# The recurrent part turned around and the Fourier part folded by symmetry, in an mLSTM cell with a Fourier mixing block

## The chip, the cores and the metric

The kernel runs on one core of a Trainium2 chip. The metric is the device time of one execution in microseconds (us). The engines are TensorE (PE in the profile, its weight loads PEld), VectorE (DVE), ScalarE (ACT), GpSimd (POOL) and SyncE (SP), which issues the DMAs.

## The reference

Two blocks in a row, all in float32. The first is a recurrent cell over 768 steps, for 4 batches and 8 heads of 40 features; the second mixes its output with a two-dimensional Fourier transform and a two-layer MLP.

```python
batch, n_heads, seq, head_dim = (4, 8, 768, 40)
for t in range(S):
    m_new = np.maximum(f_gate[:, :, t] + m, i_gate[:, :, t])
    f_stab = np.exp(f_gate[:, :, t] + m - m_new)
    i_stab = np.exp(i_gate[:, :, t] - m_new)
    m = m_new
    C = f_stab[:, :, None, None] * C + i_stab[:, :, None, None] * np.einsum('bhd,bhe->bhde', vt, kt)
    n = f_stab[:, :, None] * n + i_stab[:, :, None] * kt
    h_tilde = np.einsum('bhde,bhe->bhd', C, qt)
    nq = np.einsum('bhd,bhd->bh', n, qt)[:, :, None]
    denom = np.maximum(np.abs(nq), 1.0)
    y[:, :, t] = sigmoid(o_gate[:, :, t]) * h_tilde / denom
# x: y with the heads side by side, (4, 768, 320)
mixed = np.real(np.fft.fft(np.fft.fft(x, axis=1), axis=2))
u = x + mixed
un = (u - mean(u)) / np.sqrt(var(u) + 1e-06)          # over the 320 features
out = u + np.maximum(un @ w_ch1, 0.0) @ w_ch2         # 320 -> 1280 -> 320
```

## The kernel before

**Recurrent part** (`mlstm_chunk(b, c)`). The 768 steps of a batch are six chunks of 128. Inside a chunk the recurrence is written as a masked attention: `W` (key steps on the partitions, 8 heads times 128 query steps free) holds exp(a - M) under the causal mask, is multiplied by the scores `ps` = k·q, and `ph` = W·v1 is the part from within the chunk, v1 being v with a column of ones (so that the 41st column is nq). What came before the chunk is carried in `C` (40 x 41 for each head) and enters through `pn` = q·C, scaled by the decay of each query step. `pc` = k·(v1 scaled) updates C. In program order a chunk is: load `qk` (two DMAs), `kvt`, `Mb` (M broadcast to all partitions, 512 KB written); VectorE subtracts, GpSimd masks with `affine_select`, ScalarE takes one exp over 1024 columns; 8 matmuls ps, heads 0, 2, 4, 6 first and then 1, 3, 5, 7; VectorE multiplies W by ps; 4 matmuls pn, 8 matmuls ph with W as the standing operand; VectorE scales and adds them to `h1`; GpSimd scales v1 to `vw`; 8 matmuls pc; VectorE updates C; then `den` (three small VectorE operations), `so` times den on GpSimd, and `x` = h1 times so on VectorE.

**Fourier part** (the first half of `fnet(b)`). The sequence transform uses the sum and difference of the two halves of the sequence (`eo`, on GpSimd) for the even and the odd frequencies (`par`). `pz` and `pzt` multiply them by the table `ds_sb` (cosines beside sines, 386 or 384 columns), for the feature blocks of 128, 128 and 64; only frequencies up to 384 are computed, and copies in reverse order, the sine part negated, fill the mirrored ones into `Z` and `Zt`. The feature transform `pu` multiplies Z and Zt by `dd_sb`, five matmuls for each of six row blocks. `u` = pu + x, with its mean and variance by `bn_stats`.

**MLP** (second half of `fnet(b)`). `put` transposes u, `pm` multiplies it by the first layer (60 instructions in a group of three row blocks), ScalarE and VectorE take the relu in turn, `po` multiplies by the second layer, and the result is stored. The mean is taken out of the weights themselves (`center_weights`, matmul `pw`), and the third feature block is padded to 128 rows with zeros. The weights come as 64-bit floats and are converted from their bits by VectorE, ScalarE and GpSimd (`load_weights`).

The order at the top level is

```python
mlstm(0)
load_tables()
load_weights(cp); center_weights()
mlstm(1)
for b in range(B):
    if 1 < b + 1 < B:
        mlstm(b + 1)
    fnet(b)
```

and the framework's scheduler orders each engine's instructions at build time, by its own costs and by buffers that come free; so chunks of one batch stand between the transforms of another. All engines work their queues in that order. PSUM has four pools of two buffers each: `ps_s` for ps; `ps_h` for pn, ph and pc; `ps_f` for pz, pzt, pu and put; `ps_m` for pm, po and pw. `kvt` and `Mb` have three buffers, `qk` three, `W` two.

Of the kernel before, what the change touches and what calls it, by code (L numbers as in the profile page):

```python
# [10 lines left out]
FP = mybir.dt.float32  # L11
# [7 lines left out]
L = 128  # L19
# [7 lines left out]
TAIL = DM - 2 * L  # L27
TG = NT // 2
HALF = S // 2
NE = HALF // 2 + 1  # L30
NO = HALF // 2
M_INIT = -1.0e30
MASKED = -1.0e4


def backwards(ap, start, n):

    return bass.AP(tensor=ap.tensor, offset=ap.offset + start, ap=[list(ap.ap[0]), [-1, n]])
# [3 lines left out]
def kernel(  # L42
# [19 lines left out]
    mbp = ctx.enter_context(tc.tile_pool(name="mbp", bufs=3))  # L62
    wp = ctx.enter_context(tc.tile_pool(name="wp", bufs=2))
# [21 lines left out]
    C_bufs = [const.tile([L, NP, 2, D1], FP, name=f"C{n}") for n in range(2)]  # L85
    M_d = dram.tile([NT, BH, L], FP, name="M_d")


    with tc.tile_pool(name="gates", bufs=1) as gp:
# [11 lines left out]
        for t in qk_bufs + C_bufs:  # L101
            nc.gpsimd.memset(t, 0.0)

# [23 lines left out]
        nc.scalar.activation(out=g, in_=g, func=AF.Exp)  # L127
        dec = gp.tile([BH, BH // 2, NT], FP, name="dec")
        nc.vector.tensor_tensor(out=dec, in0=g[:, :, L - 1].unsqueeze(1).to_broadcast([BH, BH // 2, NT]),
                                in1=spread_sb[:, L:].unsqueeze(2).to_broadcast([BH, BH // 2, NT]), op=OP.mult)  # L130
        for c in range(NT):
            pt = ps_h.tile([L, 3, BH], FP, name="pt", tag="ph")
            for j, src in enumerate((a, wk, g)):
                nc.tensor.transpose(pt[:, j, :], src[:, c, :], ident[0:BH, 0:BH])
            nc.vector.tensor_copy(out=colT[:, c], in_=pt)
# [63 lines left out]
    def mlstm_chunk(b, c):  # L199
# [3 lines left out]
        C = C_bufs[b % 2]  # L203
# [5 lines left out]
        v1 = kvt[:, H * D:].rearrange("p (h d) -> p h d", d=D1)  # L209
# [4 lines left out]
        nc.vector.tensor_tensor(out=W, in0=colT[:, c, 0, heads].unsqueeze(2).to_broadcast([L, H, L]), in1=Mb,  # L214
                                op=OP.subtract)
        nc.gpsimd.affine_select(out=W, in_=W, compare_op=OP.is_ge, fill=MASKED, base=0, pattern=[[0, H], [1, L]],  # L216
                                channel_multiplier=-1)
        nc.scalar.activation(out=W, in_=W, func=AF.Exp)  # L218

        for hip in range(2):  # L220
            r = slice(hip * 64, hip * 64 + D)
            ps = ps_s.tile([L, NP, L], FP, name="ps", tag="ps")
            for p in range(NP):
                nc.tensor.matmul(ps[:, p, :], qk[r, 1, p, :], qk[r, 0, p, :], start=True, stop=True)  # L224
            Wv = W.rearrange("p (pr two) t -> p pr two t", two=2)[:, :, hip, :]
            nc.vector.tensor_tensor(out=Wv, in0=ps, in1=Wv, op=OP.mult)  # L226

        h1 = tp.tile([L, H, D1], FP, name="h1", tag="h1")
        if c > 0:
            pn = ps_h.tile([L, NP, 2 * D1], FP, name="pn", tag="ph")  # L230
            for p in range(NP):
                nc.tensor.matmul(pn[:, p, :], qk[:, 0, p, :], C[:, p].rearrange("p a b -> p (a b)"),  # L232
                                 start=True, stop=True)
            nc.vector.tensor_tensor(out=h1, in0=pn.rearrange("p pr (two d) -> p (pr two) d", two=2),
                                    in1=colT[:, c, 2, heads].unsqueeze(2).to_broadcast([L, H, D1]), op=OP.mult)
        ph = ps_h.tile([L, H, D1], FP, name="ph", tag="ph")
        for h in range(H):
            nc.tensor.matmul(ph[:, h, :], W[:, h, :], v1[:, h, :], start=True, stop=True)  # L238
        if c > 0:
            nc.vector.tensor_tensor(out=h1, in0=h1, in1=ph, op=OP.add)  # L240
        else:
            nc.vector.tensor_copy(out=h1, in_=ph)

        if c < NT - 1:
            vw = tp.tile([L, H, D1], FP, name="vw", tag="vw")
            nc.gpsimd.tensor_tensor(out=vw, in0=v1, in1=colT[:, c, 1, heads].unsqueeze(2).to_broadcast([L, H, D1]),  # L246
                                    op=OP.mult)
# [4 lines left out]
            for hip in range(2):  # L252
                r = slice(hip * 64, hip * 64 + D)
                Cv = C[r, :, hip, :]
                if c == 0:
                    nc.vector.tensor_copy(out=Cv, in_=pc[r])
                else:
                    d = decB[r, b * NP:(b + 1) * NP, c].unsqueeze(2).to_broadcast([D, NP, D1])
                    nc.vector.tensor_tensor(out=Cv, in0=Cv, in1=d, op=OP.mult)
                    nc.vector.tensor_tensor(out=Cv, in0=Cv, in1=pc[r], op=OP.add)  # L260

        nq = h1[:, :, D]
        den = tp.tile([L, H], FP, name="den", tag="den")
        nc.vector.tensor_scalar(out=den, in0=nq, scalar1=-1.0, scalar2=1.0, op0=OP.mult, op1=OP.max)  # L264
        nc.vector.tensor_tensor(out=den, in0=den, in1=nq, op=OP.max)
# [27 lines left out]
    def negate(eng, out, in_):  # L293
        if eng == 0:
            nc.scalar.mul(out, in_, -1.0)
        else:
            nc.vector.tensor_scalar(out=out, in0=in_, scalar1=-1.0, scalar2=None, op0=OP.mult)

    def fnet(b):
        x, _ = xs.pop(b)  # L300
        eo = eo_p.tile([L, 2, NT // 2, DM], FP, name="eo", tag="eo")
# [4 lines left out]
        Z = [z_p.tile([L, 2, S], FP, name=f"Z{ch}", tag=f"Z{ch}", bufs=1) for ch in range(2)]  # L306
        Zt = z_p.tile([L, S], FP, name="Zt", tag="Zt", bufs=1)
# [152 lines left out]
```

## Time and profile before

| | |
|---|---|
| median of 3 runs | 694.29 us (685.64 to 694.99) |
| profiled execution | 695.05 us, its span from first to last instruction 693.2 us |
| mean granted TensorE clock | 0.916 |
| busy share of the span | PE 89%, PEld 64%, DVE 41%, ACT 16%, POOL 19% |
| DMA | 45.60 MB, mean 66 GB/s |

The profile is of one execution. Its views give the busy time of each engine, groups of instructions by source line (L214 is line 214 of the kernel before), what each engine waited for, and the instructions in order of time. A row such as `L238 PE MATMUL ph<-kvt,W 128*128 128x41 f32 x384 | 71.2, 352 | 25.8 <-DVE W L226 24.1` reads: line, engine, operation, written tile and read tiles, sizes, count, busy us in total, mean ns of one, idle time of the engine just before, and what ended it. Matmuls are pipelined, so that the durations of neighbours overlap; the distance from one start to the next is what one costs in a stream. A timeline row gives the start and the length of a run of like instructions in us.

### The profile page before, as it was taken

To read this page: it belongs to the slowest core of one execution; us is meant where nothing else is said; L and a number is where in the kernel's file an instruction comes from. 1 tells how busy PE (TensorE), PEld (TensorE's weight loads), DVE (VectorE), ACT (ScalarE), POOL (GpSimd) and SP (SyncE) were. 2 spreads that over 40 slices of the span, in tenths; PEclk is the share of its full clock that TensorE was granted. 3 is DMA by queue.
4 is the path that set the end of the run, shared out by engine and by line. 5 is a ranking of instruction groups with operands and counts; after the bars stand their busy time and mean duration, and the time that the engine had idled before them with its cause. 6 is when DMAs were issued, how large, how long until landed. Compare 5 with 4: busy or idle time off the path is not lost.

```text
span 693.2 us, 6982 instructions
## 1 busy us (share of the span) xinstructions
PE 618.7 (89%) x2756; PEld 444.9 (64%) x2756; DVE 281.4 (41%) x558; ACT 110.1 (16%) x193; POOL 128.8 (19%) x113
## 2 busy tenths in 40 slices
PE   3879444259999999999999999999989999999998
PEld 3779423147877666687766676788756656666665
DVE  6454799995556311147343121255431011331110
ACT  4110323204102401001012021001121010110010
POOL 4230366672314100014040010021300000000000
PEclk9999999856579999997599999966999999999999
DMA  7436154542234100023220010120000000000000
GB/s 225 143 106 261 45 157 137 191 143 87 82 135 139 50 10 19 10 76 107 87 102 10 1 59 1 52 74 1 1 0 1 28 1 19 10 0 1 28 0 29
DMA packets 16113, 45.60 MB, mean 66 GB/s; under 512 B 1968, under 2 KB 5264, under 8 KB 15952
## 3 DMA queue, kind: packets, MB, share of 16 engines
q1 hardware_dynamic: 16080, 45.15, 19.8%
q8 instruction: 22, 0.36, 0.2%
q14 instruction: 11, 0.09, 0.0%
HBM read 41.11 MB, written 4.03 MB: 65 GB/s over the span
## 4 chain that ended last, share of the span: by engine, by line
PE 82%; DVE 11%; issue 3%; POOL 1%; ACT 1%; DMA 1%; POOLq 0%; DVEq 0%
PE pm L363 22%; PE po L375 19%; PE pu L340 9%; PE ph L238 9%; PE ps L224 7%; PE pz L318 6%; PE pn L232 4%; PE pzt L326 2%; DVE m L183 2%; PE pc L251 2%; DVE m L187 1%; PE put L356 1%; DVE e L182 1%; DVE e L188 1%; DVE e L179 1%
## 5 line engine op out<-in xcount | busy, mean ns | idle before, releaser
L363 PE MATMUL pm<-uT,w_sb 128*128 128x384 f32 x480 | 156.6, 487 | 0.6 <-ACT uT L357 0.6
L363 PEld LDWEIGHTS pm<-uT,w_sb 128*128 128x128 f32 x480 | 90.6, 190 | 62.4 <-ACT uT L357 0.8
L375 PE MATMUL po<-w_sb,hT 128*128 128x320 f32 x480 | 130.5, 432 | 0.0
L375 PEld LDWEIGHTS po<-w_sb,hT 128*128 128x128 f32 x480 | 91.2, 190 | 38.9
L238 PE MATMUL ph<-kvt,W 128*128 128x41 f32 x384 | 71.2, 352 | 25.8 <-DVE W L226 24.1
L238 PEld LDWEIGHTS ph<-kvt,W 128*128 128x128 f32 x384 | 68.7, 268 | 33.7 <-DVE W L226 21.8
L367 DVE TENSOR_SCALAR hT<-pm 128x384 f32<-128x384 f32 x40 | 22.3, 558 | 132.1 <-PE pm L363 132.1
L224 PE MATMUL ps<-qk 40*128 40x128 f32 x384 | 69.8, 382 | 0.3 <-DMA qk<-in_qkT 0.3
L224 PEld LDWEIGHTS ps<-qk 40*128 40x128 f32 x384 | 58.2, 266 | 6.8 <-issue 3.4
L378 DVE SCALAR_TENSOR_TENSOR ot<-po,rstd,u 128x320 f32<-128x320 f32 x24 | 13.2, 551 | 115.9 <-PE po L375 115.9
L340 PE MATMUL pu<-dd_sb,Z 128*128 128x320 f32 x192 | 56.0, 434 | 0.0
L218 ACT ACTIVATE W<-W 128x1024 f32<-128x1024 f32 x24 | 25.3, 1058 | 176.7 <-POOL W L216 176.6
L318 PE MATMUL pz<-ds_sb,eo 128*128 128x386 f32 (+1 forms) x96 | 48.1, 645 | 0.3 <-issue 0.3
L216 POOL TENSOR_SCALAR_AFFINE_SELECT W<-W 128x1024 f32<-128x1024 f32 x24 | 27.7, 1157 | 106.5 <-DVE den L264 62.2
L340 PEld LDWEIGHTS pu<-dd_sb,Z 128*128 128x128 f32 x192 | 36.1, 190 | 15.4 <-issue 0.6
L246 POOL TENSOR_TENSOR vw<-kvt,colT 128x328 f32<-128x328 f32 x20 | 15.9, 800 | 157.6 <-issue 127.1
L150 PE MATMUL pw<-w_sb,mean_sb 128*128 128x320 f32 x24 | 14.6, 774 | 30.6 <-POOL w_sb L189 23.9
L369 ACT ACTIVATE hT<-pm 128x384 f32<-128x384 f32 x40 | 19.6, 491 | 117.2 <-PE pm L363 117.2
L268 POOL TENSOR_TENSOR so<-so,den 128x320 f32<-128x320 f32 x24 | 21.0, 876 | 77.4 <-DVE den L266 77.4
L232 PEld LDWEIGHTS pn<-C,qk 128*128 128x128 f32 x160 | 31.4, 288 | 6.2 <-issue 4.9
L232 PE MATMUL pn<-C,qk 128*128 128x82 f32 x160 | 34.2, 384 | 0.5 <-DVE C L260 0.5
L226 DVE TENSOR_TENSOR W<-ps,W 128x512 f32<-128x512 f32 x48 | 32.2, 684 | 5.3 <-ACT W L218 2.8
(89 smaller groups left out, 504.9 us busy)
## 6 DMA issues: line engine op xcount, KB each, us to landing
Mb<-M_d SPq DMA_DIRECT2D x24, 512.0 KB
kvt<-in_kv SPq DMA_DIRECT2D x24, 324.0 KB
qk<-in_qkT SPq DMA_DIRECT2D x48, 160.0 KB
raw<-in_w SPq DMA_DIRECT2D x9, 640.0 KB
so<-in_o SPq DMA_DIRECT2D x4, 960.0 KB
out<-ot SPq DMA_DIRECT2D x24, 160.0 KB
ds_sb<-in_dft_s SPq DMA_DIRECT2D x1, 1155.0 KB
dd_sb<-in_dft_d SPq DMA_DIRECT2D x1, 800.0 KB
```

The costliest lines, as they stand in the source:

```text
L216: nc.gpsimd.affine_select(out=W, in_=W, compare_op=OP.is_ge, fill=MASKED, base=0, pattern=[[0, H], [1, L]], channel_multiplier=-1)
L218: nc.scalar.activation(out=W, in_=W, func=AF.Exp)
L224: nc.tensor.matmul(ps[:, p, :], qk[r, 1, p, :], qk[r, 0, p, :], start=True, stop=True)
L226: nc.vector.tensor_tensor(out=Wv, in0=ps, in1=Wv, op=OP.mult)
L232: nc.tensor.matmul(pn[:, p, :], qk[:, 0, p, :], C[:, p].rearrange("p a b -> p (a b)"), start=True, stop=True)
L238: nc.tensor.matmul(ph[:, h, :], W[:, h, :], v1[:, h, :], start=True, stop=True)
L268: nc.gpsimd.tensor_tensor(out=sc, in0=sc, in1=den.unsqueeze(2).to_broadcast([L, H, D]), op=OP.mult)
L318: nc.tensor.matmul(pz.rearrange("p a k -> p (a k)"), eo[:, par, j, ch * L:(ch + 1) * L], ds_sb[:, j, c0:c0 + 2 * n], start=(j == 0), stop= ...
L340: nc.tensor.matmul(pu, z, dd_sb[:, n, :], start=(n == 0), stop=(n == 4))
L363: nc.tensor.matmul(pu, w1_sb[:, ch, f * L:(f + 1) * L], uT[:, ch].rearrange("p c t -> p (c t)"), start=(ch == 0), stop=(ch == 2))
L367: nc.vector.tensor_scalar(out=ht, in0=pu, scalar1=0.0, scalar2=None, op0=OP.max)
L375: nc.tensor.matmul(po, hT[f][:, i * L:(i + 1) * L], w2_sb[:, f, :], start=(f == 0), stop=(f == NFF - 1))
```

## The change

Recurrent part:

- `W` is made in another order: ScalarE takes exp(a - M) straight from `Mb`, head by head (eight activations of 128 columns, a as the bias), and GpSimd's mask follows and fills with 0. VectorE's subtraction goes.
- The ps matmuls alternate between the two halves of the partitions (p outside, hip inside), into two PSUM tiles.
- `ph` is turned around: features on the partitions (two heads in 64 each), query steps free. v1, padded with zeros from 41 to 64 columns, is the standing operand, W the moving one. The old pn is added into the same PSUM tile: `C` (now 128 x 128 blocks, two alternating buffers a batch parity) stands, and `qg` moves, which is q times the decay (GpSimd), the decay broadcast by two new DMAs a chunk (`Gb`, from `G_d` in device memory). h1's scale and add on VectorE go.
- ScalarE copies ph to SBUF, four transposes on TensorE turn it back (`px`), and den and x read px.
- The product of C and its decay moves from VectorE to GpSimd.

Fourier part:

- `fe`: VectorE adds and subtracts feature d and feature 320 - d of eo, so that the cosine part has 161 features and the sine part 159. pz takes 128 of each (193 or 192 columns instead of 386 or 384), pzt the remaining 64 rows of each, alternating.
- `Z` has half its size. Mirrored frequencies are copied without negation; `dd_sb` holds the sine blocks with both signs instead.
- pu takes three matmuls for each row block instead of five.

The diff, cut to its core:

```diff
+    gbp = ctx.enter_context(tc.tile_pool(name="gbp", bufs=2))
...
-    colT = const.tile([L, NT, 3, BH], FP, name="colT")
+    colT = const.tile([L, NT, 2, BH], FP, name="colT")
+    fe = const.tile([L, 2, NT // 2, 2 * PAD], FP, name="fe")
-    C_bufs = [const.tile([L, NP, 2, D1], FP, name=f"C{n}") for n in range(2)]
+    C_bufs = [const.tile([L, NP, L], FP, name=f"C{n}") for n in range(4)]
+    G_d = dram.tile([NT, BH, L], FP, name="G_d")
...
+        nc.gpsimd.memset(fe, 0.0)
+        nc.sync.dma_start(out=G_d.rearrange("c p t -> p c t"), in_=g)
...
-        kvt = kvp.tile([L, H * (D + D1)], FP, name="kvt", tag="kvt")
+        kvt = kvp.tile([L, H * (D + VP)], FP, name="kvt", tag="kvt")
...
-        nc.vector.tensor_tensor(out=W, in0=colT[:, c, 0, heads].unsqueeze(2).to_broadcast([L, H, L]), in1=Mb,
-                                op=OP.subtract)
-        nc.gpsimd.affine_select(out=W, in_=W, compare_op=OP.is_ge, fill=MASKED, base=0, pattern=[[0, H], [1, L]],
+        for h in range(H):
+            nc.scalar.activation(out=W[:, h, :], in_=Mb[:, h, :], func=AF.Exp, scale=-1.0,
+                                 bias=colT[:, c, 0, b * H + h:b * H + h + 1])
+        nc.gpsimd.affine_select(out=W, in_=W, compare_op=OP.is_ge, fill=0.0, base=0, pattern=[[0, H], [1, L]],
                                 channel_multiplier=-1)
-        nc.scalar.activation(out=W, in_=W, func=AF.Exp)
+        ps = [ps_s.tile([L, NP, L], FP, name=f"ps{hip}", tag="ps") for hip in range(2)]
+        for p in range(NP):
+            for hip in range(2):
+                r = slice(hip * 64, hip * 64 + D)
+                nc.tensor.matmul(ps[hip][:, p, :], qk[r, 1, p, :], qk[r, 0, p, :], start=True, stop=True)
         for hip in range(2):
-            r = slice(hip * 64, hip * 64 + D)
-            ps = ps_s.tile([L, NP, L], FP, name="ps", tag="ps")
+            Wv = W.rearrange("p (pr two) t -> p pr two t", two=2)[:, :, hip, :]
+            nc.vector.tensor_tensor(out=Wv, in0=ps[hip], in1=Wv, op=OP.mult)
+        ph = ps_h.tile([L, NP, L], FP, name="ph", tag="ph")
+        if c > 0:
+            Gb = gbp.tile([L, NP, L], FP, name="Gb", tag="Gb")
+            for hip in range(2):
+                nc.sync.dma_start(out=Gb[hip * 64:hip * 64 + 64],
+                                  in_=G_d[c, b * H + hip:(b + 1) * H:2, :].unsqueeze(0).to_broadcast([64, NP, L]))
+            qg = gbp.tile([L, NP, L], FP, name="qg", tag="qg")
+            nc.gpsimd.tensor_tensor(out=qg, in0=qk[:, 0], in1=Gb, op=OP.mult)
             for p in range(NP):
-                nc.tensor.matmul(ps[:, p, :], qk[r, 1, p, :], qk[r, 0, p, :], start=True, stop=True)
...
+                nc.tensor.matmul(ph[:, p, :], C[:, p, :], qg[:, p, :], start=(p == 0), stop=False,
+                                 skip_group_check=True)
+        for p in range(NP):
+            for hip in range(2):
+                nc.tensor.matmul(ph[hip * 64:hip * 64 + 64, p, :], v1[:, 2 * p + hip, :], W[:, 2 * p + hip, :],
+                                 start=(c == 0 and p == 0), stop=True, skip_group_check=True)
+        hT = tp.tile([L, NP, L], FP, name="h", tag="h")
+        nc.scalar.copy(out=hT, in_=ph)
+        px = ps_h.tile([L, NP, L], FP, name="px", tag="ph")
+        for p in range(NP):
+            nc.tensor.transpose(px[:, p, :], hT[:, p, :], ident)
+        h1 = px.rearrange("p pr (two e) -> p (pr two) e", two=2)
...
-                    nc.vector.tensor_tensor(out=Cv, in0=Cv, in1=d, op=OP.mult)
+                    nc.gpsimd.tensor_tensor(out=Cv, in0=C[r, :, m], in1=d, op=OP.mult)
                     nc.vector.tensor_tensor(out=Cv, in0=Cv, in1=pc[r], op=OP.add)
...
+        nc.vector.tensor_copy(out=fv[:, :, 0:HALF_D + 1:HALF_D], in_=ev[:, :, 0:HALF_D + 1:HALF_D])
+        nc.vector.tensor_tensor(out=fv[:, :, 1:HALF_D], in0=near, in1=far, op=OP.add)
+        nc.vector.tensor_tensor(out=fv[:, :, PAD:PAD + HALF_D - 1], in0=near, in1=far, op=OP.subtract)
...
-            for ch in range(2):
-                pz = ps_f.tile([L, 2, n], FP, name="pz", tag="pf")
-                for j in range(NT // 2):
-                    nc.tensor.matmul(pz.rearrange("p a k -> p (a k)"), eo[:, par, j, ch * L:(ch + 1) * L],
-                                     ds_sb[:, j, c0:c0 + 2 * n], start=(j == 0), stop=(j == NT // 2 - 1))
-                copy(ch, Z[ch][:, :, k_dir], pz)
-                copy(ch, Z[ch][:, 0, k_mir], backwards(pz[:, 0, :], last, nm))
-                negate(ch, Z[ch][:, 1, k_mir], backwards(pz[:, 1, :], last, nm))
-            pz = ps_f.tile([L, n], FP, name="pzt", tag="pf")
+            pz = ps_f.tile([L, 2, n], FP, name="pz", tag="pf")
             for part in range(2):
                 for j in range(NT // 2):
-                    nc.tensor.matmul(pz[part * 64:part * 64 + TAIL], eo[:, par, j, 2 * L:DM],
+                    nc.tensor.matmul(pz[:, part, :], fe[:, par, j, part * PAD:part * PAD + L],
                                      ds_sb[:, j, c0 + part * n:c0 + (part + 1) * n],
                                      start=(j == 0), stop=(j == NT // 2 - 1))
...
+            copy(0, Z[:, :, k_dir], pz[:, :, 0:NO])
+            copy(1, Z[:, :, k_mir], backwards(pz, n - 1, NO))
+            pz = ps_f.tile([L, 1, n], FP, name="pzt", tag="pf")
+            for j in range(NT // 2):
+                for part in range(2):
+                    nc.tensor.matmul(pz[part * 64:(part + 1) * 64, 0, :], fe[:, par, j, part * PAD + L:(part + 1) * PAD],
...
-            for n, z in enumerate((Z[0][:, 0, m], Z[0][:, 1, m], Z[1][:, 0, m], Z[1][:, 1, m], Zt[:, m])):
-                nc.tensor.matmul(pu, z, dd_sb[:, n, :], start=(n == 0), stop=(n == 4))
+            for n, z in enumerate((Z[:, 0, m], Z[:, 1, m], Zt[:, 0, m])):
+                nc.tensor.matmul(pu, z, dd_sb[:, n + 2 if mir and n else n, :], start=(n == 0), stop=(n == 2))
```

More of the change, by code (lines that the diff above doesn't have):

```diff
@@ L27 @@
 TAIL = DM - 2 * L
+VP = 64
 TG = NT // 2
@@ L31 @@
 NO = HALF // 2
+HALF_D = DM // 2
+PAD = L + 64
 M_INIT = -1.0e30
-MASKED = -1.0e4
 def backwards(ap, start, n):
-    return bass.AP(tensor=ap.tensor, offset=ap.offset + start, ap=[list(ap.ap[0]), [-1, n]])
+    return bass.AP(tensor=ap.tensor, offset=ap.offset + start, ap=[list(d) for d in ap.ap[:-1]] + [[-1, n]])
 @with_exitstack
@@ L228, in mlstm_chunk @@
[L228 to L242, printed above, removed]
+        ps = [ps_s.tile([L, NP, L], FP, name=f"ps{hip}", tag="ps") for hip in range(2)]
[3 more added lines that the diff above has]
+                nc.tensor.matmul(ps[hip][:, p, :], qk[r, 1, p, :], qk[r, 0, p, :], start=True, stop=True)
```

68 lines of the change are left out of this document (35 added, 33 removed).

## The prediction

> **What bounds the kernel now.** The page's totals come first, for the engine that is full; then the busy time by stage, cut where TensorE's work changes. The columns of a stage are its length, busy time (and instructions) of PE, PEld, DVE, ACT and POOL, then TensorE's granted clock, DMA share and GB/s.
>
> ```profile
> PE 618.7 (89%) x2756; PEld 444.9 (64%) x2756; DVE 281.4 (41%) x558; ACT 110.1 (16%) x193; POOL 128.8 (19%) x113
> ```
>
> ```profile
> 14.00:79.00 65.00, 54.94 (x311) 50.79 (x310) 31.69 (x67) 7.67 (x8) 13.31 (x14) 1.00 0.43 151
> 79.00:147.00 68.00, 21.26 (x69) 13.50 (x69) 66.05 (x86) 20.67 (x25) 42.25 (x27) 0.91 0.50 157
> 147.00:208.30 61.30, 61.23 (x335) 49.08 (x335) 36.05 (x76) 13.41 (x18) 22.05 (x19) 0.63 0.31 103
> ...
> 302.00:353.80 51.80, 51.33 (x310) 39.49 (x308) 29.74 (x68) 7.85 (x14) 15.28 (x15) 0.70 0.30 98
> ...
> 446.00:495.00 49.00, 49.00 (x322) 40.91 (x321) 28.29 (x68) 5.87 (x12) 9.06 (x11) 0.72 0.13 38
> ...
> 598.50:617.00 18.50, 17.79 (x71) 12.38 (x72) 8.18 (x22) 1.51 (x7) 0.00 (x0) 1.00 0.00 1
> ```
>
> Stage A, 14 to 79 us, is the recurrent part of batch 0, with TensorE busy 54.94 of 65 us. B, to 147, converts the weights: VectorE is busy 66.05 of 68.00 us and TensorE waits. C (61.3 us), D (51.8) and E (49.0) each mix a recurrent batch with the sequence DFT of another, and TensorE has no gap. A last DFT runs alone, F, from 588.01 to 598.5. After each DFT comes a pu stage (the last row is the fourth) and an MLP stage, which the change leaves alone. So A, C, D, E, F and pu shorten as far as TensorE's work does.
>
> What that work costs is read from TensorE's timeline, from start to start: a chunk in A, a chunk in E, the last DFT.
>
> ```profile
> 53.91 0.65 PE L238 MATMUL ph<-kvt,W 128*128 128x41 f32 x2 [0.25 <-DVE W L226]
> 54.49 1.65 PE L224 MATMUL ps<-qk 40*128 40x128 f32 x6
> 56.06 3.21 PE L238 MATMUL ph<-kvt,W 128*128 128x41 f32 x14
> 59.20 0.78 PE L251 MATMUL pc<-vw,kvt 128*40 128x41 f32 x16
> 59.91 2.08 PE L224 MATMUL ps<-qk 40*128 40x128 f32 x10
> 61.92 2.00 PE L232 MATMUL pn<-C,qk 128*128 128x82 f32 x8
> 63.71 0.56 PE L238 MATMUL ph<-kvt,W 128*128 128x41 f32 x2
> ```
>
> ```profile
> 446.25 1.71 PE L224 MATMUL ps<-qk 40*128 40x128 f32 x16
> 447.89 1.12 PE L232 MATMUL pn<-C,qk 128*128 128x82 f32 x8
> 448.85 0.35 PE L238 MATMUL ph<-kvt,W 128*128 128x41 f32 x2
> 449.13 0.48 PE L224 MATMUL ps<-qk 40*128 40x128 f32 x2
> 449.55 1.76 PE L238 MATMUL ph<-kvt,W 128*128 128x41 f32 x14
> 451.23 0.51 PE L251 MATMUL pc<-vw,kvt 128*40 128x41 f32 x16
> 451.67 2.08 PE L224 MATMUL ps<-qk 40*128 40x128 f32 x14
> ...
> 588.01 3.41 PE L318 MATMUL pz<-ds_sb,eo 128*128 128x386 f32 x10
> 591.35 1.58 PE L326 MATMUL pzt<-ds_sb,eo 128*64 128x193 f32 x12
> 592.86 4.14 PE L318 MATMUL pz<-ds_sb,eo 128*128 128x384 f32 x12
> ```
>
> A matmul is two instructions here, so x16 is 8 matmuls. A chunk in A takes 9.8 us (53.91 to 63.71): ps 1.57+2.01, ph 0.58+3.14, pc 0.71, pn 1.79. In E the same takes ps 1.64, ph 0.28+1.68, pc 0.44, pn 0.96: 5.0 us. So A runs slow though its clock column reads 1.00; I go by the matmuls. C, D and E alternate, and their 0.63, 0.70 and 0.72 lie between a half and a whole.
>
> **The change, part by part.** *Recurrent part on TensorE.* ps alternates partitions 0 to 39 with 64 to 103, into two PSUM tiles. In ph, v1 (64 columns) stands and W (128) moves, in alternating output halves. pn becomes 4 matmuls of C on qg; 4 transposes come on top. Do halves overlap? pc alternates them now: x16 in 0.44 us is 28 ns each, where ps's 1.64/16 = 103 ns for 128 columns gives 33 ns for 41. pzt takes 1.51/12 = 126 ns for 193 columns, where pz's 3.34/10 = 334 ns for 386 gives 167. So yes, in part. The bounds for ps and ph are the whole time and half of it; I take half, nearest to pc, whose order is theirs. A slow chunk becomes ps 1.8, inter 1.8 (pn's row; 8 times ps's slow 0.2 would be 1.6), ph 1.8 (ps's columns, halved), transposes 4 x 0.22 = 0.9 (twice the 0.66/6 below), pc 0.7: **7.0 us**. A fast one: 0.8+1.0+0.8+0.45+0.44 = **3.5**. Saved: 2.8 slow, 1.5 fast.
>
> *Fourier part.* A batch's pz falls from 24 instructions of 386 columns to 24 of 193; pzt keeps its 24, in alternating halves; pu falls from 60 to 36.
>
> ```profile
> 550.80 0.66 PE put L356 x6
> ...
> 598.50 16.36 PE pu L340 x60
> ```
>
> pu: 24 fewer at 16.36/60 = 273 ns are 6.55 us, in four batches **26 us**, on the path. What is left, 9.8 us, still covers VectorE's 8.18 us of the stage. pz and pzt at full clock: 24 x 334 + 24 x 126 = 11.0 us become 24 x 167 + 24 x (84 to 126) = 6.0 to 7.0; I take 6.5, so 0.41 goes.
>
> *Other engines.*
>
> ```profile
> L318 PE MATMUL pz<-ds_sb,eo 128*128 128x386 f32 (+1 forms) x96 | 48.1, 645 | 0.3 <-issue 0.3
> L326 PE MATMUL pzt<-ds_sb,eo 128*64 128x193 f32 (+1 forms) x96 | 17.5, 391 | 0.0
> L214 DVE TENSOR_TENSOR W<-colT,Mb 128x1024 f32<-128x1024 f32 x24 | 30.2, 1258 | 2.5 <-DMA Mb<-M_d 2.5
> L216 POOL TENSOR_SCALAR_AFFINE_SELECT W<-W 128x1024 f32<-128x1024 f32 x24 | 27.7, 1157 | 106.5 <-DVE den L264 62.2 <-DVE W L214 20.2 <-DVE den L266 13.7
> L218 ACT ACTIVATE W<-W 128x1024 f32<-128x1024 f32 x24 | 25.3, 1058 | 176.7 <-POOL W L216 176.6
> L268 POOL TENSOR_TENSOR so<-so,den 128x320 f32<-128x320 f32 x24 | 21.0, 876 | 77.4 <-DVE den L266 77.4
> L246 POOL TENSOR_TENSOR vw<-kvt,colT 128x328 f32<-128x328 f32 x20 | 15.9, 800 | 157.6 <-issue 127.1 <-PE pc L251 25.7 <-DVE colT L135 4.2
> L259 DVE TENSOR_TENSOR C<-C,decB 40x164 f32<-40x164 f32 x32 | 12.0, 376 | 0.4
> L234 DVE TENSOR_TENSOR h<-pn,colT 128x328 f32<-128x328 f32 x20 | 9.9, 496 | 16.6 <-PE pn L232 16.6
> L358 ACT COPY uT<-put 64x128 f32<-64x128 f32 x24 | 6.2, 258 | 0.0
> L102 POOL MEMSET qk<- 128x1024 f32 x3 | 2.8, 962 | 0.1
> ```
>
> In a chunk VectorE loses L214, L234, the sum of h with ph (of L234's shape) and two L259: 1.26+0.50+0.50+0.75 = 3.0 us. ScalarE swaps one exp of 1.06 us for eight of 128 columns (bounds 0.13 us each, an eighth of L218, and 0.26, L358; I take 0.26, so 2.1) and gets a copy of 512 columns, by L218's rate at least 0.5, I take 0.6: +1.6. GpSimd gains qg, 512 columns at vw's 2.44 ns = 1.25 us, and two products for C of 164 = 0.8 us: from 1.16+0.80+0.88 = 2.8 to **4.9 us**. Beside TensorE's 7.0 that is hidden, beside 3.5 it is the bound. The fold adds two sums of 954 columns a batch on VectorE, by L214 about 2.4 us: beside the MLP for batches 1 to 3, in C for batch 0, where its 36 us lose 16. Uncovered it is 2.4 us a batch. Z needs fewer copies. Preparing gives GpSimd 3320 more columns of memset, at 962 ns per 1024 3.1 us, inside its 4.2 us wait for colT (L246).
>
> *The added waits.* The transposes wait for ScalarE's copy of ph. On TensorE the next chunk's ps, and in C, D and E a piece of pz, can stand between; else it idles 0.6 us, and 2.1 more if eight exps stand ahead of the copy. px holds one of the two ph buffers through den, so and x. I allow 2 us in A and 3 us in each of C, D, E.
>
> *DMA.* kvt grows by 92 KB and Gb adds 256 KB a chunk: A's 151 GB/s over 65 us, 9.8 MB, become 11.7 MB in 51 us, 229 GB/s, by A's ratio a share near 0.65. SP gets two more issues a chunk, behind Mb in its queue, and Gb's buffers free only when qg has read them; a late one holds the next chunk's qk and kvt loads, which run up to three chunks ahead. I count it hidden.
>
> *Stage B* keeps its VectorE and GpSimd conversion; the chunk and a half in it frees 4 us of VectorE and takes 3 of GpSimd: -1.
>
> **Sum.** Chunks by stage are ps instructions through 16:
>
> ```profile
> 147.00:208.30 61.30, 15.53 (x88) 0.63 0.31 103
> 302.00:353.80 51.80, 12.53 (x76) 0.70 0.30 98
> 446.00:495.00 49.00, 13.31 (x80) 0.72 0.13 38
> ```
>
> C has 5.5, D 4.75, E 5; A 6 and B 1.5 of the 24; the rest stand beside the MLP. pz and pzt took 65.6 us, less F's 10.5 are 55 in C, D, E; 0.41 of it is 22.5, 7.5 in each. By the clock a chunk saves 2.4 us in C and 2.2 in D and E. A: 6 x 2.8 - 2, less the missing pn and pc: -14. C: 5.5 x 2.4 + 7.5 - 3: -18. D: 4.75 x 2.2 + 7.5 - 3: -15. E: 5 x 2.2 + 7.5 - 3: -15. F: -4. pu: -26. The one and a quarter chunks beside the MLP, fast: -2. B: -1. Together -95 on the profiled execution's 695.05 us (span 693.2): **600 us**. The median shown, 694.29, lies 0.8 below that execution.
>
> **Rivals.** F, pu, the MLP chunks and B, -33 in all, are in each.
>
> *Clock up* (0.15): the new matmuls move 128 columns in both halves, and TensorE runs fast throughout, as at 446 us. Then GpSimd binds: A 6 x 4.9 + the 10 us in which TensorE now waits = 40; C 22+5.5 x 2.1 = 34, D 28, E 27 with handoffs: -25-27-24-22-33 = 564 us. For it: E's first chunk is fast behind dense work. Against: A is slow with TensorE 85% busy.
>
> *Clock down* (0.17): gaps keep it slow. C 5.5 x 7.0 + 2 x 6.5 = 51, D 46, E 48, A as forecast: -14-10-6-1-33 = 631. [...]
>
> *No overlap* (0.09): the halves take turns, and the change doesn't do what it says. A slow chunk is 3.6+1.8+3.2+0.9+0.7 = 10.2 us, a fast one 5.2. A +4, C -4, D -4, E -4 (pz and pzt save 0.36), rest -33: 654. [...]
>
> *Loop through GpSimd* (0.11): a chunk's select stands in the queue behind the last one's so: select 1.2, product 1.4, ph 1.8 to 3.7, copy 0.6, transposes 0.9, den 0.8, so 0.9, handoffs 1: about 10 us. A 60, C 55, D 48, E 50: -5-6-4+1-33 = 648. Against: the same loop has been there, and a chunk in A went at TensorE's 9.8 us.
>
> *Slower* (0.04): the same queue, and nothing overlaps; with exps 2.1 and x 0.7 it is 13.4 us a chunk. A 80, C 74, D 64, E 67: 58 more than their 227.1, less 33, is 720. It decides from a cycle of (227+33)/21.25 = 12.2 us. Against: W has two buffers, so exp and select can run a chunk ahead, and GpSimd has 2 us a chunk free.
>
> **Numbers.** Forecast, 580 to 620: 0.44. The range, 562 to 655, reaches to clock up and to the cases near 650; a spread of some us around those and the slower case leave out 2 in 10. Within 2%, about what a measurement of this kernel can tell from no change, would need the recurrent part to grow by some 40 us against the 55 that pu, F, the MLP chunks and the pz share give: faster 0.92, same 0.04, slower 0.04.
>
> **What would show it.** Right: pu x36 in 9.8 us; ps x16 under 2 us where slow; A near 51 us, C 43, D 37, E 34; MLP stages unmoved. Wrong: TensorE idle behind the copy of ph (ScalarE) or px's buffer (GpSimd's so); ps still above 3 us where slow; B longer.

## The result, and the profile after

The changed kernel took 633.0 us in the median of 4 runs (627.98 to 635.97), beside 694.55 us for the kernel before on the same chip: a ratio of 0.913, 95% interval 0.904 to 0.923. (Times are medians of all executions; the ratios are formed apart and leave out executions more than 1.5% above the fastest of their kernel, so that the two can differ a little.) The forecast was 600 us, a gain of 95; the gain was 61.5. The profiled execution took 635.97 us, its span is 634.3 us.

The totals of the page after, the line that answers to the first of before:

```profile
PE 535.2 (84%) x2750; PEld 372.2 (59%) x2750; DVE 225.0 (35%) x450; ACT 152.4 (24%) x366; POOL 166.5 (26%) x168
```

TensorE lost 83.5 busy us, but its share fell from 89 to 84%: some of what it lost came back as waiting. Where, is read from the moment at which the first pm of each batch starts, since the MLP behind it was left alone:

| stretch, by the two timelines of TensorE | before | after | measured | forecast |
|---|---|---|---|---|
| start to pm of batch 0 | 229.12 | 219.33 | -9.8 | -39.5 (A, B, C, one pu) |
| to pm of batch 1 | 143.53 | 125.58 | -18.0 | -22.5 (D, pu, chunks beside the MLP) |
| to pm of batch 2 | 142.48 | 122.16 | -20.3 | -22.5 (E, pu, chunks) |
| to pm of batch 3 | 102.04 | 91.22 | -10.8 | -10.5 (F, pu) |
| to the end of the profiled execution | 77.88 | 77.68 | -0.2 | 0 |

So 30 of the 36 us that are missing are missing before the first MLP. The busy times by stage, columns as before (length, PE, PEld, DVE, ACT, POOL, then granted clock, DMA share, GB/s):

```profile
14.00:79.00 65.00, 51.27 (x332) 41.40 (x332) 16.02 (x42) 18.88 (x55) 21.92 (x27) 0.79 0.56 179
79.00:147.00 68.00, 19.76 (x44) 11.50 (x44) 64.91 (x81) 25.11 (x42) 44.67 (x27) 0.50 0.47 146
147.00:197.50 50.50, 43.61 (x364) 35.11 (x364) 21.89 (x50) 15.13 (x42) 25.11 (x28) 0.76 0.51 167
292.00:330.70 38.70, 33.99 (x347) 27.00 (x346) 19.61 (x48) 17.75 (x50) 26.63 (x30) 1.00 0.65 192
418.80:455.00 36.20, 33.37 (x355) 26.93 (x353) 18.53 (x52) 11.67 (x33) 21.37 (x25) 1.00 0.21 67
```

The last two rows are D and E. They reach past the first wait of pu; up to the first pu, where D and E of the kernel before end, both are 33.1 us long (to 325.12 and 451.92) where 37 and 34 were forecast. They got there in another way: TensorE ran at full clock. Of the 4.7 and 2.8 us in which it is not busy in these rows, 3.7 and 1.2 are pu waiting for Zt. A fills its 65 us still and goes on to 82 us.

The timeline of TensorE in one chunk of A, from one inter-chunk product to the next:

```profile
62.21 2.08 PE L248 MATMUL ph<-qg,C 128*128 128x128 f32 x8 [2.78 <-POOL qg L246]
64.22 0.69 PE L252 MATMUL ph<-W,kvt 128*64 128x128 f32 x2
64.84 1.22 PE L233 MATMUL ps<-qk 40*128 40x128 f32 x4
65.99 1.97 PE L252 MATMUL ph<-W,kvt 128*64 128x128 f32 x14
67.89 1.65 PE L233 MATMUL ps<-qk 40*128 40x128 f32 x8
69.47 1.11 PE L258 MATMUL px<-ident,h 128*128 128x128 f32 x4
70.51 0.78 PE L268 MATMUL pc<-vw,kvt 128*40 128x41 f32 x16
71.21 0.80 PE L233 MATMUL ps<-qk 40*128 40x128 f32 x4
74.31 2.08 PE L248 MATMUL ph<-qg,C 128*128 128x128 f32 x8 [2.29 <-POOL qg L246]
```

From 62.21 to 74.31 it is 12.1 us: inter 2.01, ph 0.62 + 1.90, ps 1.15 + 1.58 + 0.80, px 1.04, pc 0.70, together 9.8, and 2.3 of waiting for qg. The 9.8 us are just what a chunk in A took before. What held qg before 62.21 stands in GpSimd's timeline:

```profile
59.14 0.99 POOL L276 TENSOR_TENSOR C<-C,decB 40x164 f32<-40x164 f32 x2 [7.41 <-DVE C L277]
60.22 0.72 POOL L284 TENSOR_TENSOR so<-so,den 128x320 f32<-128x320 f32 x1
60.90 1.26 POOL L246 TENSOR_TENSOR qg<-qk,Gb 128x512 f32<-128x512 f32 x1
62.11 1.09 POOL L225 TENSOR_SCALAR_AFFINE_SELECT W<-W 128x1024 f32<-128x1024 f32 x1
```

GpSimd has time to spare (7.41 us idle), but the next chunk's qg and select stand in its queue behind C's product, which itself waits for VectorE's C, and behind so.

The last Fourier transform begins, pu begins, and pu ends where put begins:

```profile
539.61 1.80 PE L337 MATMUL pz<-ds_sb,fe 128*128 128x193 f32 x10
...
546.01 1.34 PE L361 MATMUL pu<-dd_sb,Z 128*128 128x320 f32 x4
...
555.80 0.49 PE L377 MATMUL put<-ident,u 128*128 128x128 f32 x3
```

pu takes 9.79 us (546.01 to 555.80; 9.8 was forecast), pz and pzt together 6.4 (539.61 to 546.01; 6.5 was forecast). These were the well-sized parts.

For batch 0 and 1 the stage of pu nevertheless kept its length (from first pu to first pm 20.9 us before and 21.8 after in batch 0, 18.9 and 19.8 in batch 1). VectorE's timeline in batch 0's, and then in batch 1's, shows the fold of the next batch:

```profile
206.79 1.04 DVE L321 COPY fe<-eo 128x12 f32<-128x12 f32 x1 [2.77 <-POOL eo L314]
207.75 1.14 DVE L322 TENSOR_TENSOR fe<-eo 128x954 f32<-128x954 f32 x1
208.81 0.48 DVE L362 TENSOR_TENSOR u<-pu,x 128x320 f32<-128x320 f32 x1
...
327.18 1.23 DVE L321 COPY fe<-eo 128x12 f32<-128x12 f32 x1 [2.27 <-POOL eo L314]
328.31 2.10 DVE L322 TENSOR_TENSOR fe<-eo 128x954 f32<-128x954 f32 x1
330.33 0.34 DVE L307 COPY Zt<-pzt 128x192 f32<-128x192 f32 x1
```

VectorE's queue stands at fe until GpSimd has made eo (4.4 us); behind it wait the u that empties pu's PSUM buffer (TensorE idle 3.6 us) and the copy of Zt that pu reads (3.7 us). From the waits of TensorE (us in total, times, longest), the rows of these two and of qg:

```profile
PE ph L248 <- POOL qg L246: 5.7, 3, 2.8
PE pu L361 <- DVE Zt L307: 4.9, 2, 3.7
...
PE pu L361 <- DVE u L362: 3.6, 1, 3.6
```

### The profile page after: what moved, and what is told of

Its sections match the earlier page's. It is cut to its first block, busy times and chain, and to the rows that moved or that the text cites. A ratio compares the mean times of both kernels' runs of the same rounds, so it can differ in the third digit from the quotient of the medians.

```text
span 634.3 us, 7201 instructions
## 1 busy us (share of the span) xinstructions
PE 535.2 (84%) x2750; PEld 372.2 (59%) x2750; DVE 225.0 (35%) x450; ACT 152.4 (24%) x366; POOL 166.5 (26%) x168
## 4 chain that ended last, share of the span: by engine, by line
PE 59%; POOL 3%; DVE 2%; issue 1%; ACT 1%; POOLq 0%
PE pm L384 25%; PE po L396 20%; PE pu L361 5%; PE ps L233 2%; PE ph L252 2%; PE pz L337 1%; PE put L377 1%; POOL eo L314 1%; PE px L258 1%; POOL so L284 1%; PE ph L248 1%; PE pc L268 1%; POOL C L276 1%; DVE fe L322 1%; POOL vw L263 1%
## 5 line engine op out<-in xcount | busy, mean ns | idle before, releaser
L384 PEld LDWEIGHTS pm<-uT,w_sb 128*128 128x128 f32 x480 | 90.7, 190 | 62.5 <-ACT uT L378 0.8
L252 PE MATMUL ph<-W,kvt 128*64 128x128 f32 x384 | 41.5, 334 | 27.5 <-DVE W L236 26.7
L233 PE MATMUL ps<-qk 40*128 40x128 f32 x384 | 61.6, 355 | 1.9 <-DMA qk<-in_qkT 1.9
L223 ACT ACTIVATE W<-Mb,colT 128x128 f32<-128x128 f32 x192 | 59.4, 390 | 3.8 <-DMA Mb<-M_d 2.6
L233 PEld LDWEIGHTS ps<-qk 40*128 40x128 f32 x384 | 47.6, 233 | 14.3 <-issue 11.1
L252 PEld LDWEIGHTS ph<-W,kvt 128*64 128x64 f32 x384 | 30.2, 167 | 35.1 <-issue 22.5
L255 ACT COPY h<-ph 128x512 f32<-128x512 f32 x24 | 14.0, 584 | 137.6 <-PE ph L252 137.5
L361 PE MATMUL pu<-dd_sb,Z 128*128 128x320 f32 x96 | 32.9, 468 | 8.7 <-DVE Zt L307 4.9
L378 ACT COPY uT<-put 128x256 f32<-128x256 f32 x24 | 8.9, 370 | 115.9 <-PE put L377 115.8
L248 PE MATMUL ph<-qg,C 128*128 128x128 f32 x160 | 28.0, 330 | 10.0 <-POOL qg L246 5.7
L248 PEld LDWEIGHTS ph<-qg,C 128*128 128x128 f32 x160 | 24.4, 232 | 13.4 <-POOL qg L246 6.9
```

The lines of the kernel that those rows point to most:

```text
L223: nc.scalar.activation(out=W[:, h, :], in_=Mb[:, h, :], func=AF.Exp, scale=-1.0, bias=colT[:, c, 0, b * H + h:b * H + h + 1])
L233: nc.tensor.matmul(ps[hip][:, p, :], qk[r, 1, p, :], qk[r, 0, p, :], start=True, stop=True)
L248: nc.tensor.matmul(ph[:, p, :], C[:, p, :], qg[:, p, :], start=(p == 0), stop=False, skip_group_check=True)
L252: nc.tensor.matmul(ph[hip * 64:hip * 64 + 64, p, :], v1[:, 2 * p + hip, :], W[:, 2 * p + hip, :], start=(c == 0 and p == 0), stop=True, sk ...
L361: nc.tensor.matmul(pu, z, dd_sb[:, n + 2 if mir and n else n, :], start=(n == 0), stop=(n == 2))
L384: nc.tensor.matmul(pu, w1_sb[:, ch, f * L:(f + 1) * L], uT[:, ch].rearrange("p c t -> p (c t)"), start=(ch == 0), stop=(ch == 2))
```

## The experiments

Three theories had to be told apart for the missing part: the halves do not overlap; GpSimd's queue (C, so, qg, select, one after the other) sets the chunk; TensorE's clock, taken to follow the work in it, is the cause. Each kernel was timed beside the kernel before; its profile is of one execution.

**Each half of the change alone.** The first keeps the old recurrent part and takes the folded Fourier part; the second the reverse.

> The kernel before with the Fourier part of the change alone (fold, smaller pz, pu with three matmuls). Theory: pu gives 26 us, F 4 and the pz and pzt of C, D and E about 22, but each fold stands in VectorE's queue ahead of the last copy of Zt and of u, and TensorE waits for it as it does in the changed kernel (about 4, 8 and 6 us in C, D and E): about 660 us. Rival 1: the folds hide when the recurrent part is the old one, whose own work keeps TensorE busy: 643 us. Rival 2: the Fourier part is all of the gain: 633 us.

> The changed kernel with the old Fourier part, so the recurrent part of the change alone. Theory: it gains in D and E, where TensorE is fast and pz fills its gaps, about 10 us each, a few us in C, nothing in A: 665 to 672 us, with A as long as before (about 67 us). Rival: the recurrent part gains nothing anywhere, what D and E gained is the Fourier part: 690 us or more.

Fourier alone: 682.7 us, ratio 0.983 (0.970 to 0.995), above all three values expected. Recurrent alone: 667.4 us, 0.960 (0.949 to 0.971), as its theory said. By the ratios, single gains of about 12 and 28 us stand against 60 for both: the parts are far from adding up. The windows of the Fourier part alone, in C (pu starts at 218.9; two rows), D and E; the profiled execution, 685.07 us, is among the longest of its four (674.1 to 685.4):

```profile
147.00:200.00 53.00, 45.65 (x245) 41.41 (x245) 30.96 (x56) 9.65 (x8) 17.34 (x15) 0.50 0.24 80
200.00:218.80 18.80, 18.80 (x87) 15.98 (x86) 8.34 (x19) 2.12 (x5) 5.16 (x5) 0.55 0.32 109
310.00:352.50 42.50, 42.50 (x311) 35.76 (x310) 23.80 (x53) 3.60 (x6) 8.26 (x10) 0.92 0.33 103
440.00:500.50 60.50, 58.68 (x333) 51.53 (x331) 31.03 (x69) 5.46 (x7) 11.24 (x13) 0.58 0.14 40
```

With the old recurrent matmuls (41 or 82 columns) and half of pz gone, C ends 10.7 us later than before the change, at half clock, and in its last 18.8 us TensorE has no gap. As the fastest execution of this kernel is 11 us shorter than the profiled one, that length need not hold for all. E has become 11.5 us longer at 0.58; D went the other way, 9.3 us shorter at 0.92. The rows of the granted clock in 40 slices, of before, Fourier alone and recurrent alone, in this order, show where the slow slices lie:

```profile
PEclk9999999856579999997599999966999999999999
```

```profile
PEclk9999999555556879999899999955589999999999
```

```profile
PEclk9999999955899999999999999997989999999999
```

The fold alone makes more slices slow, early and late; the new recurrent part alone has hardly any in the later batches (its profile, too, is of a longer execution: 671.30 us of 659.8 to 673.0). The first slices read 9 in these kernels although ps took 0.2 us an instruction there, where it takes 0.11 in fast stretches, so A is judged by its matmuls: half clock, said of A, means that they take about twice their fast time.

**More of the old dense work.** To Fourier alone, each pz is issued a second time and overwrites the first: 96 more instructions of 193 columns.

```diff
-            for part in range(2):
+            for part in (0, 1, 0, 1):
```

> The Fourier part alone, with every pz matmul issued twice (the second time overwrites the first with the same), so TensorE has 96 instructions of 193 columns more, 16 us at full clock and 32 us at half. Theory: the Fourier part alone gained only 9 to 12 us because pz was the dense work that raised the clock in C, D and E, and with half of it these stages run slow (0.50 in most of C); with the work put back as mere load the clock comes back, and the time stays within 8 us of the Fourier part alone, 674 to 690 us, or falls. Rival, the clock does not depend on it: 16 to 32 us more, 699 to 715 us.

687.8 us, ratio 0.987 (0.979 to 0.994): 5.1 us more by the medians and about 3 by the ratios, where 96 instructions at 167 ns are 16 us and at half clock 32. The difference lies within the scatter of both, so that it bounds the cost rather than measures it. The added work cost less than its own time. The end of C shows how. Up to 205 us TensorE's timelines of the two kernels run alike, at half clock (both read 0.50 from 147 to 200 us); then come the last pz of C, first in Fourier alone, then with pz twice:

```profile
212.35 4.21 PE L331 MATMUL pz<-ds_sb,fe 128*128 128x192 f32 x12
```

```profile
211.99 4.17 PE L331 MATMUL pz<-ds_sb,fe 128*128 128x192 f32 x24
```

Twice the instructions take the same time, at full clock instead of half (170 ns an instruction from start to start against 345), and TensorE is without a gap in both. It is not so everywhere: E reads 0.58 without and 0.77 with the added work (440 to 500 us), but D, which reads 0.92 without, has slow matmuls with it: 14 instructions of ph took 3.13 us there (315.79 to 318.92) against 1.69 without (342.94 to 344.63). So more of pz can bring the clock up, and these two profiles do not say when it does.

**The halves of ps in turn**, so that less of ps can overlap.

```diff
-        for p in range(NP):
-            for hip in range(2):
+        for hip in range(2):
+            for p in range(NP):
```

> The changed kernel with the ps matmuls of one partition half after the other, as before, instead of alternating. Theory: alternating the partition halves never made them overlap (8 instructions take 0.86 us where fast and 1.58 where slow, 107 and 197 ns each, as before), so nothing changes: 633 us within 1.5%, and ps unchanged. Rival: the alternation does save something, and the time rises by 24 chunks times 0.8 to 1.6 us: 652 to 670 us.

630.3 us, 0.915 (0.908 to 0.921): nothing lost. I first read this as "ps does not overlap". That was wrong, as the filler kernels below showed: in the built program the framework's scheduler issues a ps matmul when its PSUM buffer comes free, and of 192 ps matmuls of the changed kernel only 65 stand right behind one of the other half; 66 stand behind one of their own and 61 behind other work. The alternation is in the source and hardly in the queue. Written in turn, 33 of 192 still stand behind one of the other half, so the two kernels differ by less than they seem to.

**The edges moved between engines.** Alone: ph's copy from ScalarE to VectorE; C's product and qg from GpSimd to VectorE; all three; those and so; and the fold's two sums from VectorE to GpSimd with the small copy on ScalarE.

```diff
-        nc.scalar.copy(out=hT, in_=ph)
+        nc.vector.tensor_copy(out=hT, in_=ph)
...
-            nc.gpsimd.tensor_tensor(out=qg, in0=qk[:, 0], in1=Gb, op=OP.mult)
+            nc.vector.tensor_tensor(out=qg, in0=qk[:, 0], in1=Gb, op=OP.mult)
...
-        nc.vector.tensor_tensor(out=fv[:, :, 1:HALF_D], in0=near, in1=far, op=OP.add)
+        nc.gpsimd.tensor_tensor(out=fv[:, :, 1:HALF_D], in0=near, in1=far, op=OP.add)
```

> The changed kernel with the copy of ph on VectorE instead of ScalarE. Theory: in stage A a chunk takes about 12 us because the queues tie it into a loop, and one knot is ScalarE, where the eight exps of the next chunk stand behind the copy of this one; untied, A falls by about 10 us, C and D by some: 615 to 622 us. Rival: A is bound by TensorE at its slow clock, so the time stays at 630 to 636 us and A at about 68 us.

> The changed kernel with the product of C and its decay and the product qg on VectorE instead of GpSimd, whose work on a chunk falls from 4.9 to 2.8 us. Theory: the other knot of the loop is GpSimd, where the select of a chunk stands behind C products, so and qg of the one before (TensorE waited 5.7 us for qg alone); untied, the time falls to 615 to 622 us. Rival, TensorE at its slow clock: 630 to 636 us.

> The changed kernel with the copy of ph, the C product and qg all on VectorE. Theory of the two knots: both gains, 603 to 615 us, stage A near 52 us. Rival, TensorE at its slow clock: 630 us, with stage A above 62 us and TensorE nearly without gaps in it. Second rival, VectorE becomes the knot (3.0 us a chunk more): above 636 us.

> The changed kernel with the copy of ph, the C product, qg and, beyond the last such run, the product so on VectorE, so that GpSimd has only the select and vw of a chunk (and eo), and ScalarE only the exps. Theory: what was left of the loop in A is the select, which stood in GpSimd's queue behind so of the chunk before (so at 62.1 us, select at 62.8, 12 us a chunk), although its exps were done at 48.3; with so gone the select runs a chunk ahead, a chunk in A falls from 12 to 9 us or less (TensorE's slow work is 8.9), A ends near 72 us instead of 85, and the time is 612 to 622 us. Rival: the cycle stays 12 us because TensorE's own order (ps halves between ph and px) holds it: A as before, 630 to 637 us.

> The changed kernel with the two sums of the fold on GpSimd instead of VectorE, and its small copy on ScalarE. Theory: TensorE waited at the end of C, D and E because the fold of the next batch held VectorE's queue, ahead of u and of the last copy of Zt; off that queue it costs nothing there: 615 to 622 us. Rival: the 4.4 us more on GpSimd delay the recurrent part's select and so, and the pu stage starts no sooner: 633 us or more.

| moved | us | ratio (95%) | last x of A starts |
|---|---|---|---|
| changed kernel | 633.0 | 0.913 (0.904 to 0.923) | 81.92 |
| copy | 645.6 | 0.926 (0.921 to 0.932) | 81.86 |
| C and qg | 633.6 | 0.910 (0.906 to 0.915) | 84.36 |
| copy, C, qg | 635.4 | 0.913 (0.907 to 0.918) | 84.53 |
| copy, C, qg, so | 632.2 | 0.911 (0.902 to 0.921) | 81.74 |
| fold on GpSimd | 637.5 | 0.921 (0.910 to 0.932) | 74.31 |

No move gains by itself: each of the five came out near its rival's value or above it, the copy above both values named for it (TensorE waited 8.6 us for u and 5.5 for the copy there). With so on VectorE too, GpSimd's select runs ahead, and still TensorE waits 2.30 us in a chunk (ph L248 at 62.88), now for VectorE's qg. So GpSimd's queue alone does not set A's length. With the fold on GpSimd, pu's waits fall from 8.5 us to 0.7, but those of ph for W rise from 26.7 to 30.4, behind the select, as the rival had it. There the profiled execution had a faster A, whose code is that of the changed kernel, and was also the fastest (628.46 us; the other three took 637.4 to 638.2): executions of one kernel differ by some 9 us here, a profile is of one of them, and A can run faster in one without any edit to it.

**The best of these together**: copy, C, qg and so on VectorE, ps in turn, the fold's sums on GpSimd.

> The same with the fold on GpSimd, which has room now, its small copy on ScalarE, and the ps matmuls in turn. Theory: the pu stages of batches 0, 1 and 2 lose their waits behind the fold (4, 4 and 3 us), ps in turn gives up to 3 us as it did alone: 8 to 12 us less than the run before it, 602 to 612 us. Rival: GpSimd's 4.4 us of fold a batch take the place of the waits, and nothing is gained.

621.0 us (618.6 to 622.4), 0.898 (0.892 to 0.905), 11 us below the same without the last two moves, the step that was expected (602 to 612 had been worked out from 612 to 622 for the run before, which took 632). With VectorE's queue free of the fold, pu no longer waits for u (6.8 us in the run before) or Zt; what ps in turn gave of the 11 was not separated. The first pu is at 192.2 instead of 197.5, but A still ends with its last x at 81.90.

**The clock, by itself.** Two matmuls of 512 columns are added to each chunk of batch 0, whose product nobody reads; first to the changed kernel, then to the last version.

```diff
+        if b == 0:
+            for n in range(2):
+                wm = ps_m.tile([L, NP * L], FP, name="warm", tag="pm")
+                nc.tensor.matmul(wm, ident, qk[:, n].rearrange("p a t -> p (a t)"), start=True, stop=True)
```

> The changed kernel, with two matmuls of 128 x 128 on 512 columns added to each of the six chunks of stage A (batch 0), their product read by nobody. By the rows of the Fourier part each costs 0.89 us at full clock and 1.77 us slow. Theory: stage A runs slow because its matmuls are short and leave gaps of 2 to 3 us a chunk; dense work keeps the clock up, ps 8 instructions falls from 1.57 to 0.86 us and a chunk from 12 us to 7 to 10 us although it holds 1.8 us more: stage A ends 12 to 30 us earlier, and the time is 605 to 621 us. Rival: TensorE's rate in A has nothing to do with what fills it, and the added matmuls only cost: 1.5 to 3.5 us a chunk, A ends 9 to 20 us later, 640 to 655 us. In between (time within 5 us of the changed kernel's): the gaps take the added work and the clock stays where it is.

> The version with copy, product of C, qg and so on VectorE, ps in turn and the fold's sums on GpSimd (621.0 us, stage A ending at 82.4 us), with the filler in stage A besides. In the profiled execution of the changed kernel with filler, stage A ended at 73.9 us instead of 82.4 and the first pu began 8.5 us earlier, but its median fell only by 3 us. Theory: stage A is TensorE at a clock that dense work raises, and in this version no GpSimd wait is left in its way: A ends near 70 to 75 us and the whole is 8 to 12 us shorter, 609 to 613 us. [...]

On the changed kernel: 630.1 us, 0.915 (0.905 to 0.925), no difference that the time can show, though in the profiled execution (626.9 us, its fastest) the last x of A starts at 73.45 instead of 81.92. As A reached 74.31 with the fold on GpSimd and no filler, that one profile does not show the filler's effect. On the last version: **608.1 us** (604.4 to 611.5, six runs), 0.877 (0.871 to 0.882), where no run of it without filler was below 618.6. The last x of A starts at 70.95 instead of 81.90, the first pu at 177.17 instead of 192.21. Twelve useless matmuls, at 0.9 to 2.0 us each, make the kernel 13 us faster. TensorE's timeline in A of the last version, without filler:

```profile
56.04 1.97 PE L252 MATMUL ph<-W,kvt 128*64 128x128 f32 x14
57.94 2.07 PE L233 MATMUL ps<-qk 40*128 40x128 f32 x8
```

and with it:

```profile
39.13 1.13 PE L232 MATMUL warm<-qk,ident 128*128 128x512 f32 x2
40.18 1.09 PE L256 MATMUL ph<-W,kvt 128*64 128x128 f32 x14
41.20 1.13 PE L232 MATMUL warm<-qk,ident 128*128 128x512 f32 x2
42.16 0.60 PE L262 MATMUL px<-ident,h 128*128 128x128 f32 x4
42.69 0.51 PE L272 MATMUL pc<-vw,kvt 128*40 128x41 f32 x16
43.13 1.71 PE L237 MATMUL ps<-qk 40*128 40x128 f32 x16
44.85 1.13 PE L252 MATMUL ph<-qg,C 128*128 128x128 f32 x8
```

The 14 instructions of ph take 1.90 us without (56.04 to 57.94), 1.02 with it (40.18 to 41.20). Without the filler ph is slow in four of the six chunks of A and partly slow in two; with it, slow in the fifth and partly in the second. The filler also moves the order (ps no longer stands between ph and px), so a part of the 11 us that A loses may be the order's; the instructions themselves are faster. In both filler kernels TensorE now waits for the load of Mb (1.89 and 1.43 us before the ph at 45.67 and 47.41 us), which the prediction had counted as hidden. The changed kernel with filler, whose ps stands in full alternation at this point of the queue, settles the first theory:

```profile
41.53 1.16 PE L237 MATMUL ps<-qk 40*128 40x128 f32 x16
42.62 1.16 PE L252 MATMUL ph<-qg,C 128*128 128x128 f32 x8
```

Sixteen in 1.09 us alternating (41.53 to 42.62), 1.72 in turn (43.13 to 44.85), both at full clock (px of the same chunk takes 0.53 us in each, where it takes 1.04 without filler at 59.94): halves of ps do overlap, to 0.63 of the time, where the queue lets them.

## Why the prediction was right, and where it failed

Direction and mechanism held: TensorE bounds the kernel, and C, D, E, F and the later pu stages, in which it has less to do, are shorter. The time is 33 us above the forecast, near the 631 us of "clock down" by another route: that rival had D and E at 46 and 48 us and A at 51; D and E took 33.1 each at full clock, and A kept its 65. The nearness is luck. One of the prediction's own signs of being wrong came: ps takes 3.5 us where slow, above its 3. By its steps:

- **pu, F, pz**: pu 9.79 us against 9.8, pz and pzt 6.4 against 6.5. Of the -26 for pu, batches 2 and 3 got theirs (their stages lost 5.0 and 6.5 us); batches 0 and 1 lost it again to the fold.
- **The fold** was counted as hidden on VectorE. Its work is small (L322 took 1.14 and 2.10 us); what the step missed is its place in an in-order queue, ahead of u and Zt and itself waiting for eo. "Uncovered it is 2.4 us a batch" priced the busy time and not the wait. Taken out of that queue it gained nothing alone; with ps in turn, in the kernel whose GpSimd had been relieved, it was worth 11 us.
- **The halves**: "I take half, nearest to pc". ph did come down, at full clock to 64 ns an instruction (16 in 1.03 us, from 306.80), where ps in turn takes 107 for as many columns. For ps the term of 1.8 us measured 3.5 in a chunk of A: overlap is real (0.63, not a half), but in the built queue only a third of ps stands behind the other half. Where two halves of 40 rows do alternate, these traces show 1.6 times the speed (1.09 us against 1.72 for sixteen).
- **The slow chunk**, 7.0 us in the sum, measured 9.8: ps +1.7, ph +0.7, inter +0.2, px +0.1. With 2.3 us of waiting, where 2 us had been allowed for the whole stage, a chunk of A is 12.1. **This is the failed step**: A was to give 14 us. Its last x and VectorE's first conversion operation, which begins B, are before and after:

```profile
76.25 0.49 DVE L179 TENSOR_SCALAR e<-raw 128x640 uint32<-128x640 uint32 x1
82.83 1.82 DVE L269 TENSOR_TENSOR x<-h,so 128x320 f32<-128x320 f32 x1
```

```profile
81.92 0.49 DVE L285 TENSOR_TENSOR x<-px,so 128x320 f32<-128x320 f32 x1 [0.84 <-POOL so L284]
82.32 0.48 DVE L186 TENSOR_SCALAR e<-raw 128x640 uint32<-128x640 uint32 x1
```

The last x is 0.9 us earlier, and B begins 6 us later, since the conversion now stands in the queue behind it. What one slow chunk was to save, 2.8 us, it did not save at all.
- **B** is then 4.4 us shorter (first conversion operation to the last correction of w_sb: 69.4 and 65.0), against -1. **C** gave 12.3 (62.5 to 50.2) of 18. Together with the 0.9 of pu's stage, 6.0 - 4.4 - 12.3 + 0.9 = -9.8, where -39.5 was forecast.
- **The clock** was held where it was in C, D and E, with both ways out as rivals. It rose to 1.00 in D and E, where a chunk takes 5.4 us (307.83 to 313.21) against a fast 3.5 in the sum, ps alone 1.8 against 0.8. That error and the clock cancelled: D and E came near their forecast by luck. In C it rose to 0.76. In A it stayed low for the later chunks (0.64 from 48 to 62 us, 0.50 from there to 79, with ps at 197 ns an instruction at 67.89). "Clock up" put A at GpSimd's 4.9 us a chunk; with filler, where the column reads 0.98 (14 to 48 us), a chunk took 7.0 us, filler included (34.05 to 41.09 in the changed kernel with it).
- **The rival through GpSimd** (648 us) had the queue right, select behind so, and the wait is there in A. But taking it away did not shorten A: at half clock TensorE's own 9.8 us come first, and the wait moves to the next engine (2.30 us for VectorE's qg).

What the terms of the sum hid: they were added as if independent. The clock ties them. With the fold alone it fell in C (0.63 before, 0.50 and 0.55 then) and E (0.72 before, 60.5 us at 0.58 then) and rose in D (0.70 to 0.92); with the new recurrent part alone D and E read 1.00 and 0.95. That the fold's missing work lowers it and the new matmuls raise it is the likely reading; the runs do not give the rule. A clock that rises with how busy TensorE is would fit the filler kernels (14 instructions of ph in 1.02 us with the filler, 1.90 without); C of the kernel before (61.23 of 61.30 us busy at 0.63) and of the Fourier part alone (18.80 of 18.80 at 0.55) speak against it, if busy means occupied. What in TensorE's work the clock follows, no run here tells; why A runs at half clock stays open with it.

One count of the prediction is off without consequence: preparing adds 3696 columns of memset by the tiles (2304 for fe, 1392 for C), not 3320.

## What to carry to other kernels

Price a stage of short matmuls at full and at half clock (ps took 107 and 197 ns an instruction here), not at the clock of the stage before the change alone, and expect two edits that change what TensorE does there not to add up (12 and 28 us alone, 60 together). An overlap that the source writes down must be looked for in the built queue (65 of 192 here), and an added operation is priced by what stands behind it in its engine's queue while it waits (pu lost 3.6 and 3.7 us behind the fold). Where a stage on the critical path runs at half clock and has gaps, a filler matmul into an unused buffer is a cheap test, and may be a gain (13 us here, and none that the time can show in the changed kernel itself).

## What was not expected of the hardware

- Useless work can pay: twelve matmuls of 512 columns took the best version from 621.0 to 608.1 us.
- TensorE without a gap can run near half clock (18.80 of 18.80 us at 0.55 in the Fourier part alone), and with gaps at full clock (33.37 of 36.20 us at 1.00 in E after the change).
- Two halves of ps in alternation took 68 ns an instruction against 107 in turn; the transposes, 4 instructions, took 0.58 us behind a ps of 109 ns an instruction (46.47 us after the change) and 1.04 behind one of 197 (69.47), so they slow down with it.
- The same sum over 954 columns on VectorE took 1.14 us in batch 0's stage and 2.10 in batch 1's, there beside a select and a product qg of GpSimd, which took 1.99 us where the one before it took 1.26. In batch 0's stage GpSimd was the slower one instead (vw 1.72 us against 0.74, qg 2.17). Each slow one ran beside an operation of the other engine; whether the two hinder each other was not tried by itself.
